# The small products of the last 64 rows for keys and queries, laid side by side on the array's row halves

## The chip, the cores and the metric

The kernel runs on one core of a Trainium2 chip. The metric is the time of one execution on the device in microseconds (us): before the change, the median of three runs is 894.02 us.

## The reference, cut to what matters

Two layers of the same pair of blocks work on x, a 2048 x 448 fp32 matrix:

```python
def _A_ref(x, wqkv, wo):                 # x has been through _layernorm
    q, k, v = (x @ wqkv) ...             # three 448 x 448 projections, 16 heads of 28
    phi = lambda t: where(t > 0, t + 1, exp(t)) + 1e-6
    kv  = einsum("bhsd,bhse->bhde", phi(k), v)
    z   = einsum("bhsd->bhd", phi(k))
    num = einsum("bhqd,bhde->bhqe", phi(q), kv)
    den = einsum("bhqd,bhd->bhq", phi(q), z) + 1e-6
    return (num / den) @ wo
def _B_ref(x, w1, b1, w2, b2):
    return gelu(x @ w1 + b1) @ w2 + b2   # 448 -> 1792 -> 448
x = x + _A_ref(_layernorm(x), ...);  x = x + _B_ref(_layernorm(x), ...)   # twice
```

The change touches only how phi(k) and phi(q) get their projections, x @ wqkv for keys and queries.

## The kernel before, in words

**Numbers in two pieces.** Every fp32 operand of a product is split into a high piece `hi` (a rounding copy to fp32r) and a low piece `lo` (what the rounding left), and a product is taken as hi·hi + hi·lo + lo·hi. The 2048 rows of x are cut into 16 tiles of 128 rows, numbered t. The 448 columns of x, which are the contraction of the projections, are cut into three chunks of 128 and a tail of 64.

**The tail.** Its 64 rows are stored twice in the transposed x, in rows 0-63 and again in rows 64-127, in the high piece as well as in the low piece. The weight of the tail, `cross` (tile `wk6` or `wq6`), holds the high piece in rows 0-63 and the low piece in rows 64-127 (`split_tail`, L97 to L100). So one matmul over 128 rows with the high piece of x gives hi·hi + hi·lo (L282), and one with the low piece gives lo·hi, together with lo·lo (L283). With three matmuls for each of three chunks (L279, L280, L281), a projection of one tile is 11 matmuls of 448 columns (`proj`).

**First half of a layer (`phase1`, L471).** For each tile t the order of the instructions is written out by hand as a string of tokens, `STEP` (L455), `STEP_0` (L456) for t = 0:

```python
STEP   = "a qp K T X s n G kp tu kh bg Q sp"
STEP_0 = "K T X kp a s kh n tu G Q bg sp"
```

On TensorE this makes, per step t: K(t), the key projection (11 matmuls, `stage_k`); T(t+1), the transposes of the next tile into a PSUM bank `tp` (four transposes, L228, only in layer 0 and only up to tile 5: `TURNED = (6, 0)`, later tiles are transposed on VectorE and through DRAM); G(t-1), 11 matmuls that add phi(k)ᵀx (L435 to L439); Q(t), the query projection (11 matmuls, `stage_q`), for t below `DEFER` = 10 only; the last six query projections stand between the two halves of a layer. The other engines follow each bank: `qp` is phi of the query of the step before, two ScalarE activations (L289, L290) and one VectorE instruction that I call eq(t-1) (L292, tile `eq`), which is the last to read the query's bank; `X` splits the transposed tile, ScalarE for the high piece XH (L234) and then VectorE for the low piece XL (L235), which K(t+1) reads; `a` and `n` are layer norm of tiles further on (L177 to L183, L356); `kp`, `kh` are phi of the key and its split.

**PSUM banks.** A pool tag has a fixed number of bank buffers. Tag "h" has two and is used by the query projection `psq` (L274) and by the transposes `tp` of layer 0; tag "m" has two and holds the key projection; tag "acc" has four and holds G. A new tile of a tag takes the buffer that came free first, and its first writer waits for the last reader of the buffer's old contents. Before the change, `psq` of step t takes the bank of `psq` of step t-1, and waits for eq(t-1); `tp` of tile t+1 takes the bank of `tp` of tile t.

The second half of a layer (the combination with wo and the MLP: `hp` L699 to L703, `y` L717 to L719) holds most of the time, is on TensorE as well, and isn't touched.

Of the kernel before, what the change touches and what calls it, by code (L numbers as in the profile page):

```python
# [10 lines left out]
F32R = mybir.dt.float32r  # L11
# [11 lines left out]
def linear_attn_mlp_kernel(  # L23
# [12 lines left out]
    pe, act, dve, pool, sp = nc.tensor, nc.scalar, nc.vector, nc.gpsimd, nc.sync  # L36
    x0 = x_in[0]
    y_out = out[0]
    S, D = x0.shape
# [22 lines left out]
    def bank(tag, bufs, name):  # L62
        return psum.tile([128, 512], F32, name=name, tag=tag, bufs=bufs)
# [7 lines left out]
    def t512(tag, bufs, name, dt=F32):  # L71
        return work.tile([128, 512], dt, name=name, tag=tag, bufs=bufs)

    def f(ap):
        return ap.bitcast(F32)
# [10 lines left out]
    wkq = {}  # L86
# [7 lines left out]
            eng.dma_start(s[64:128], src[TL:D, :])  # L94
        return s

    def split_tail(s, cross, tmp):  # L97
        act.copy(tmp, s)
        dve.tensor_copy(cross[0:64], s[0:64])
        dve.tensor_sub(cross[64:128], s[64:128], f(tmp[64:128]))  # L100

    def load_kq(name, col):
        src = wqkv[:, col:col + D]
# [18 lines left out]
    def piece(name, i):  # L122
        return t448(f"{'W' if name == 'k' else 'V'}{i}", 1, f"w{name}{i}", F32R)

    def split_kq(name, st):
        for c in range(3):
            hi = piece(name, c)
            lo = piece(name, 3 + c)
            act.copy(hi, st[c])
            if c == (0 if name == "k" else 1):  # L130
                dve.tensor_sub(lo, st[c], f(hi))
            else:
                pool.tensor_tensor(lo, st[c], f(hi), op=OP.subtract)
            wkq[name, c] = (hi, lo)
        cr = piece(name, 6)
        split_tail(st[3], cr, t512("e", 3, "sx", F32R)[:, :D])
        wkq[name, 3] = cr

    st_k = load_kq("k", D)
# [75 lines left out]
    blocks = {}  # L215
# [54 lines left out]
        dve.tensor_sub(lo.rearrange("p (c i n) -> p c i n", c=4, n=32), x, f(h))  # L270


    def proj(name, key, j):
        ps = bank("m" if name == "k" else "h", 2, "ps" + name)  # L274
        o = ps[:, :D]
        b = blocks[key]
        for c in range(3):
            hi, lo = wkq[name, c]
            pe.matmul(o, b.still(b.hi, j, c), hi, start=(c == 0), stop=False)  # L279
            pe.matmul(o, b.still(b.hi, j, c), lo, start=False, stop=False)  # L280
            pe.matmul(o, b.still(b.lo, j, c), hi, start=False, stop=False)  # L281
        pe.matmul(o, b.still(b.hi, j, 3), wkq[name, 3], start=False, stop=False)  # L282
        pe.matmul(o, b.still(b.lo, j, 3), wkq[name, 3], start=False, stop=True)  # L283
        return o

    def phi(o, name, into=None):

        e = t512("e", 3, name)[:, :D]
        act.activation(e, o, AF.Relu, scale=-1.0)  # L289
        act.activation(e, e, AF.Exp, scale=-1.0)  # L290
        into = e if into is None else into
        dve.scalar_tensor_tensor(into, o, 0.0, e, op0=OP.max, op1=OP.add)  # L292
        return into
# [99 lines left out]
    ko = {}  # L393

    def stage_k(l, t):
        ko[l, t] = proj("k", ("a", l, t // 4), t % 4)

    def stage_kphi(l, t):
        o = ko.pop((l, t))
# [13 lines left out]
            dve.tensor_tensor(za, e, za, op=OP.add)  # L413
        ks[l, t] = (kh, kl)

    qo = []

    def stage_q(l, t):
        if t is None:
            return  # L420
        qo.append((l, t, proj("q", ("a", l, t // 4), t % 4)))

    def stage_qphi():
        while qo:
# [28 lines left out]
    DEFER = NT - ORDER.split().count("Q")  # L453
# [17 lines left out]
    def phase1(l, tr):  # L471
        za = consts.tile([128, D], F32, name="za", tag="za")
        acc = [bank("acc", 4, f"G{c}")[:, :D] for c in range(4)]
        for t in range(NT):
# [3 lines left out]
            for tok in (STEP if t else STEP_0).split():  # L478
# [4 lines left out]
                elif tok == "a":  # L483
                    for u in norm:
                        stage_a(l, u)
                elif tok == "n":
                    for u in norm:
                        stage_n(l, u)
                elif tok == "tu":
                    for u in norm:  # L490
                        stage_t(l, u)
                elif tok == "T" and t + 1 < NT:
                    stage_b(l, t + 1)
                elif tok == "X" and t + 1 < NT and (l == 0 or t + 1 >= 4):
                    stage_x(l, t + 1)
                elif tok == "K":
                    stage_k(l, t)
                elif tok == "qp":
                    stage_qphi()
                elif tok == "kp":  # L500
                    stage_kphi(l, t)
                elif tok == "kh":
                    stage_kh(l, t, za)
                elif tok == "s":
                    stage_s(l, t)
                elif tok == "G" and t >= 1:
                    stage_g(l, t - 1, acc)
                elif tok == "bg" and l == 0:
                    background(BG[t])
                elif tok == "Q" and t < DEFER:  # L510
                    stage_q(l, t)
# [297 lines left out]
    stage_a(0, 0)  # L809
    stage_n(0, 0)  # L810
    split_kq("k", st_k)
    stage_b(0, 0)
    stage_x(0, 0)
    stage_a(0, 1)
    stage_n(0, 1)
    split_kq("q", st_q)
    sp.dma_start(b1s, b1.rearrange("(c p) -> p c", p=128))
    sp.dma_start(b2b, b2[None, :].to_broadcast([128, D]))

    for l in range(LAYERS):  # L820
# [6 lines left out]
        def pre(j):  # L827
# [3 lines left out]

        tok_ = SimpleNamespace(
            Q=lambda j: stage_q(l, fill.pop(0)), Qp=lambda j: stage_qphi(), G=lambda j: stage_g(l, NT - 1, acc),
            ld=lambda j: (load_pq(l, 0, j), load_x(l, j)), z=lambda j: trans_z(tr, za), gt=lambda j: trans_gt(tr, acc),
            kv=lambda j: trans_kv(tr), mask=lambda j: trans_mask(tr), m=lambda j: trans_m(tr, j),
# [4 lines left out]
        for tok in ORDER.split():  # L840
            name, j = tok.rstrip("0123456789"), int("0" + tok.lstrip("abcdefghijklmnopqrstuvwxyzQTG"))
# [5 lines left out]
        for b in range(NB):  # L847
# [6 lines left out]
            for i in range(NF):  # L854
                if i + 1 < NF:
                    mlp1(l, b, i + 1)
                elif nxt:
                    mlp1(l, b + 1, 0)
                if l == 0 and b == 0:
                    background(1)  # L860
                if nxt:
                    behind(l, b, i, tr)
                elif l + 1 < LAYERS:
                    if i == 2:
                        split_kq("k", st_k)
                    if i == 5:
                        split_kq("q", st_q)
                    if i in (3, 4, 6, 7, 8):
                        t = (3, 4, 6, 7, 8).index(i)
                        stage_a(l + 1, t)  # L870
                        stage_n(l + 1, t)
                        stage_t(l + 1, t)
                        if t % 2:
                            stage_sp(l + 1, t)
                    if 9 <= i < 13:
                        stage_x(l + 1, i - 9)
                mlp2(l, b, i, acc)
# [28 lines left out]
```

## Time and profile before

| | |
|---|---|
| median of three runs | 894.02 us (894.0 to 894.94) |
| the profiled execution's own time | 896.46 us |
| its span, first to last instruction | 894.7 us |
| mean granted TensorE clock in it | 0.996 |
| busy: TensorE, VectorE, ScalarE, GpSimd | 98%, 56%, 38%, 23% of the span |
| first half of layer 0, steps 1 to 5 | 17.57 to 54.99 us of the span |
| first half of layer 1, steps 1 to 9 | from 457.99 us of the span |

All terms of the prediction come from the profiled execution, which is 2.4 us longer than the median. In the rows of a timeline the columns are start, duration, engine, line, operation, output <- inputs, shapes, count; a bracket at the end of a row is the idle time of that engine just before the row and what ended it. PE is TensorE's matmul, PEld its weight load, DVE is VectorE, ACT ScalarE, POOL GpSimd. A matmul's recorded duration is longer than the step from one matmul to the next, because they are pipelined; the pace is read from the starts.

### The profile page before, as it was taken

The numbers are of one execution on the slowest core, as the hardware profiler recorded it, in microseconds if no ns is written. First come the engines' busy times: TensorE is split into PE (matmuls) and PEld (weight loads), VectorE is DVE, ScalarE is ACT, GpSimd is POOL, SyncE is SP. The second block draws the span as 40 slices with busy tenths as digits, with TensorE's granted clock in tenths as the row PEclk, the third lists the DMA queues.
The fourth block names the chain that finished last, engine by engine and source line by source line (L and its number), as shares of the span: only waits on it lengthen the run. The fifth ranks groups of instructions, "written<-read, shape, count | busy, mean of one in ns | idle before, by whom it ended". The sixth has DMA issues, their size and how long they took to land.

```text
span 894.7 us, 11665 instructions
## 1 busy us (share of the span) xinstructions
PE 878.8 (98%) x4184; PEld 772.8 (86%) x4184; DVE 502.3 (56%) x970; ACT 339.5 (38%) x586; POOL 209.1 (23%) x243
## 2 busy tenths in 40 slices
PE   7999999999999999999999999999999999999998
PEld 6898988888788888888889998888878888888887
DVE  6897686655754544226469866864565473532112
ACT  4677744333222322333345564343132233223221
POOL 4576723322112012002023333320310210210000
PEclk8999999999999999999999999999999999999999
DMA  6386622623513412051135542053233223010001
GB/s 175 121 244 220 194 82 92 208 76 102 170 52 92 143 33 80 16 175 48 47 127 196 173 123 82 32 178 112 65 106 132 91 92 130 34 62 20 22 1 42
DMA packets 62762, 93.71 MB, mean 105 GB/s; under 512 B 8816, under 2 KB 57968, under 8 KB 62704
## 3 DMA queue, kind: packets, MB, share of 16 engines
q1 hardware_dynamic: 62704, 92.97, 32.9%
q8 instruction: 33, 0.54, 0.3%
q14 instruction: 25, 0.20, 0.1%
HBM read 55.65 MB, written 34.08 MB: 100 GB/s over the span
## 4 chain that ended last, share of the span: by engine, by line
PE 84%; DVE 7%; issue 2%; DMA 2%; ACT 2%; POOL 2%; SPq 1%; POOLq 0%; DVEq 0%; ACTq 0%
PE y L719 10%; PE y L717 10%; PE y L718 10%; PE hp L701 8%; PE hp L700 8%; PE hp L699 8%; PE hp L703 3%; PE hp L702 3%; PE G L436 2%; PE G L437 2%; PE G L435 2%; PE op L652 2%; PE op L651 2%; PE op L653 2%; PE psk L281 2%
## 5 line engine op out<-in xcount | busy, mean ns | idle before, releaser
L709 DVE TENSOR_TENSOR gl<-g,gh 128x512 fp32r<-128x512 f32 x112 | 78.5, 701 | 303.6 <-ACT gh L708 303.5
L705 ACT ACTIVATE g<-hp,b1s 128x512 f32<-128x512 f32 x112 | 77.1, 688 | 400.7 <-PE hp L703 400.6
L717 PE MATMUL y<-w2h,gh 128*128 128x448 f32 x448 | 163.8, 366 | 1.7 <-ACT g L705 1.7
L719 PE MATMUL y<-w2h,gl 128*128 128x448 f32 x448 | 163.8, 366 | 0.5 <-DVE gl L709 0.5
L718 PE MATMUL y<-w2l,gh 128*128 128x448 f32 x448 | 163.6, 365 | 0.0
L701 PE MATMUL hp<-XL,w1h 128*128 128x512 f32 x336 | 131.3, 391 | 0.3 <-DVE XL L270 0.3
L699 PE MATMUL hp<-XH,w1h 128*128 128x512 f32 x336 | 131.5, 391 | 0.1
L700 PE MATMUL hp<-XH,w1l 128*128 128x512 f32 x336 | 131.6, 392 | 0.0
L183 POOL TENSOR_TENSOR brs<-bve,mhalf 128x1 f32<-128x1 f32 x64 | 39.8, 622 | 320.4 <-DVE bve L181 318.3
L717 PEld LDWEIGHTS y<-w2h,gh 128*128 128x128 f32 x448 | 84.1, 188 | 11.4 <-ACT g L705 2.5
L718 PEld LDWEIGHTS y<-w2l,gh 128*128 128x128 f32 x448 | 84.1, 188 | 8.3
L719 PEld LDWEIGHTS y<-w2h,gl 128*128 128x128 f32 x448 | 84.2, 188 | 7.5 <-DVE gl L709 0.9
L701 PEld LDWEIGHTS hp<-XL,w1h 128*128 128x128 f32 x336 | 63.1, 188 | 14.8 <-DVE XL L270 1.2
L699 PEld LDWEIGHTS hp<-XH,w1h 128*128 128x128 f32 x336 | 63.1, 188 | 11.8 <-ACT XH L269 0.8
L700 PEld LDWEIGHTS hp<-XH,w1l 128*128 128x128 f32 x336 | 63.1, 188 | 11.2
L708 ACT CAST gh<-g 128x512 fp32r<-128x512 f32 x112 | 69.7, 622 | 3.6
L602 POOL TENSOR_TENSOR pz<-pq,zb 128x448 f32<-128x448 f32 x32 | 37.1, 1162 | 105.2 <-DVE dn L608 74.0
L666 POOL TENSOR_TENSOR x<-x,b2b 128x448 f32<-128x448 f32 x32 | 36.9, 1152 | 31.5 <-DVE xm L190 23.3
L702 PE MATMUL hp<-XH,w1x 128*128 128x512 f32 x112 | 43.6, 389 | 0.0
L703 PE MATMUL hp<-XL,w1x 128*128 128x512 f32 x112 | 43.6, 389 | 0.0
L177 DVE BATCH_NORM_STATS2 bst<-x 128x6 f32<-128x448 f32 x64 | 39.8, 622 | 6.3 <-DMA x<-in_A_x_dram 5.2
L389 POOL TENSOR_TENSOR xnl<-x,xnh 128x384 fp32r<-128x384 f32 x32 | 35.4, 1107 | 29.6 <-ACT xnh L388 23.0
(144 smaller groups left out, 1581.1 us busy)
## 6 DMA issues: line engine op xcount, KB each, us to landing
x<-in_A_x_dram SPq DMA_DIRECT2D x32, 224.0 KB, 4.0
pq_d<-eq SPq DMA_DIRECT2D x32, 224.0 KB, 2.2
pq<-pq_d SPq DMA_DIRECT2D x32, 224.0 KB, 3.2
x<-x_d SPq DMA_DIRECT2D x32, 224.0 KB, 3.3
sq_a<-sq SPq DMA_DIRECT2D x13, 512.0 KB, 2.6
sp<-sq_a SPq DMA_DIRECT2D x52, 128.0 KB, 3.0
sq_q<-sq SPq DMA_DIRECT2D x12, 512.0 KB, 2.6
sp<-sq_q SPq DMA_DIRECT2D x48, 128.0 KB, 3.0
```

The costliest lines, as they stand in the source:

```text
L177: dve.bn_stats(st, xs)
L699: pe.matmul(o, w1h[:, c, s], x.moving(x.hi, c), start=(c == 0), stop=False)
L700: pe.matmul(o, w1l[:, c, s], x.moving(x.hi, c), start=False, stop=False)
L701: pe.matmul(o, w1h[:, c, s], x.moving(x.lo, c), start=False, stop=False)
L702: pe.matmul(o, w1x[:, s], x.moving(x.hi, 3), start=False, stop=False)
L703: pe.matmul(o, w1x[:, s], x.moving(x.lo, 3), start=False, stop=True)
L705: act.activation(g, hp, AF.Gelu_apprx_tanh, bias=b1s[:, i:i + 1])
L708: act.copy(gh, g)
L709: dve.tensor_sub(gl, g, f(gh))
L717: pe.matmul(acc[j], gh[:, s], w2h[:, i], start=first, stop=False)
L718: pe.matmul(acc[j], gh[:, s], w2l[:, i], start=False, stop=False)
L719: pe.matmul(acc[j], gl[:, s], w2h[:, i], start=False, stop=last)
```

## The change

In steps 1 to 9 of each layer, the low-times-high product of the tail, which was one 128-row matmul for the key and one for the query, becomes a 64-row matmul for each: the key's in rows 0-63, the query's in rows 64-127, one right behind the other at the end of K(t). For that, `cross` of the queries holds its high piece in rows 64-127 (the keys' stays in rows 0-63), and lo·lo, which the 128-row form added, is no longer computed in these steps. The query's bank is therefore opened (`proj_open`, first matmul with start=True) at the end of K(t) instead of at the start of Q(t). Step 0 and the six late query projections keep the old form. The number of matmuls, and of instructions on every other engine, doesn't change.

```diff
-    def split_tail(s, cross, tmp):
+    def split_tail(s, cross, tmp, hi):
+        hi, lo = (slice(0, 64), slice(64, 128)) if hi == 0 else (slice(64, 128), slice(0, 64))
         act.copy(tmp, s)
-        dve.tensor_copy(cross[0:64], s[0:64])
-        dve.tensor_sub(cross[64:128], s[64:128], f(tmp[64:128]))
+        dve.tensor_copy(cross[hi], s[hi])
+        dve.tensor_sub(cross[lo], s[lo], f(tmp[lo]))
...
-    def proj(name, key, j):
-        ps = bank("m" if name == "k" else "h", 2, "ps" + name)
-        o = ps[:, :D]
+    def proj_open(name):
+        return bank("m" if name == "k" else "h", 2, "ps" + name)[:, :D]
+
+    def proj(name, key, j, o, lo_tail=None):
...
-        pe.matmul(o, b.still(b.hi, j, 3), wkq[name, 3], start=False, stop=False)
-        pe.matmul(o, b.still(b.lo, j, 3), wkq[name, 3], start=False, stop=True)
+        pe.matmul(o, b.still(b.hi, j, 3), wkq[name, 3], start=False, stop=lo_tail == "first")
+        if lo_tail is None:
+            pe.matmul(o, b.still(b.lo, j, 3), wkq[name, 3], start=False, stop=True)
         return o
 
+    def proj_pair(key, j, k, q):
+        b = blocks[key]
+        lo = b.still(b.lo, j, 3)
+        pe.matmul(k, lo[0:64], wkq["k", 3][0:64], start=False, stop=True)
+        pe.matmul(q, lo[64:128], wkq["q", 3][64:128], start=True, stop=False)
...
     def stage_k(l, t):
-        ko[l, t] = proj("k", ("a", l, t // 4), t % 4)
+        key, j = ("a", l, t // 4), t % 4
+        pair = 1 <= t < DEFER
+        ko[l, t] = proj("k", key, j, proj_open("k"), "last" if pair else None)
+        if pair:
+            q_open[l, t] = proj_open("q")
+            proj_pair(key, j, ko[l, t], q_open[l, t])
...
     def stage_q(l, t):
...
-        qo.append((l, t, proj("q", ("a", l, t // 4), t % 4)))
+        pair = (l, t) in q_open
+        o = q_open.pop((l, t)) if pair else proj_open("q")
+        qo.append((l, t, proj("q", ("a", l, t // 4), t % 4, o, "first" if pair else None)))
```

More of the change, by code (lines that the diff above doesn't have):

```diff
@@ L135, in split_kq @@
         cr = piece(name, 6)
-        split_tail(st[3], cr, t512("e", 3, "sx", F32R)[:, :D])
+        split_tail(st[3], cr, t512("e", 3, "sx", F32R)[:, :D], 0 if name == "k" else 1)
         wkq[name, 3] = cr
@@ L278, in proj @@
             hi, lo = wkq[name, c]
-            pe.matmul(o, b.still(b.hi, j, c), hi, start=(c == 0), stop=False)
+            pe.matmul(o, b.still(b.hi, j, c), hi, start=(c == 0 and lo_tail != "first"), stop=False)
             pe.matmul(o, b.still(b.hi, j, c), lo, start=False, stop=False)
             pe.matmul(o, b.still(b.lo, j, c), hi, start=False, stop=False)
-        pe.matmul(o, b.still(b.hi, j, 3), wkq[name, 3], start=False, stop=False)
-        pe.matmul(o, b.still(b.lo, j, 3), wkq[name, 3], start=False, stop=True)
-        return o
+        pe.matmul(o, b.still(b.hi, j, 3), wkq[name, 3], start=False, stop=lo_tail == "first")
+        if lo_tail is None:
+            pe.matmul(o, b.still(b.lo, j, 3), wkq[name, 3], start=False, stop=True)
+        return o
+    def proj_pair(key, j, k, q):
[3 more added lines that the diff above has]
+        pe.matmul(q, lo[64:128], wkq["q", 3][64:128], start=True, stop=False)
     def phi(o, name, into=None):
@@ L414, in stage_kh @@
         ks[l, t] = (kh, kl)
-    qo = []
+    qo, q_open = [], {}
     def stage_q(l, t):
```

## The prediction

> **What bounds the kernel now.** I read the page first, for the busy shares and the chain that ended last, then TensorE's timeline of the first half of layer 0, then VectorE's and ScalarE's beside it.
>
> ```profile
> span 894.7 us, 11665 instructions
> PE 878.8 (98%) x4184; PEld 772.8 (86%) x4184; DVE 502.3 (56%) x970; ACT 339.5 (38%) x586; POOL 209.1 (23%) x243
> PE 84%; DVE 7%; issue 2%; DMA 2%; ACT 2%; POOL 2%; SPq 1%; POOLq 0%; DVEq 0%; ACTq 0%
> ```
>
> TensorE is the bound: 84% of the chain. So a matmul slot taken out is worth its length, and a wait put in front of TensorE is worth its length as well, unless a later wait shrinks for it. Step 2 of layer 0 in TensorE's timeline, with the starts of the next steps:
>
> ```profile
> 28.00 0.36 PE L282 MATMUL psk<-wk,XH 128*128 128x448 f32 x1
> 28.20 0.36 PE L283 MATMUL psk<-wk,XL 128*128 128x448 f32 x1
> 28.41 0.49 PE L228 MATMUL tp<-ident,x 128*128 128x128 f32 x3
> 28.76 0.45 PE L435 MATMUL G<-kh,xnh 128*128 128x448 f32 x1
> 31.72 0.47 PE L279 MATMUL psq<-wq,XH 128*128 128x448 f32 x1 [0.47 <-DVE eq L292]
> 34.05 0.36 PE L279 MATMUL psk<-wk,XH 128*128 128x448 f32 x1
> 48.30 0.36 PE L279 MATMUL psk<-wk,XH 128*128 128x448 f32 x1
> 50.53 0.36 PE L435 MATMUL G<-kh,xnh 128*128 128x448 f32 x1
> ```
>
> The pace is 0.203 us a matmul (K(5): 11 from 48.30 to 50.53). The transposes T take 0.35 us (28.41 to 28.76). The one bracket is what matters here: Q(2) waited 0.47 us for eq(1), the last reader of the query's bank. That reader is already late by a little in layer 0.
>
> **What the change takes out.** In each of 18 steps (1 to 9, two layers) two slots, 0.406 us, become one pair. What a pair costs, the trace of before can't show: no stationary or moving tile in it has 64 rows. The weight loads bound it:
>
> ```profile
> 31.71 0.19 PEld L279 LDWEIGHTS psq<-wq,XH 128*128 128x128 f32 x1 [0.85 <-DVE eq L292]
> 31.82 0.19 PEld L280 LDWEIGHTS psq<-wq,XH 128*128 128x128 f32 x1
> 28.01 0.19 PEld L283 LDWEIGHTS psk<-wk,XL 128*128 128x128 f32 x1
> ```
>
> From below: the two run in one slot with both loads hidden, 0.203. From above: each runs quite alone, load 0.19 and record 0.36, 1.10 for the two. In between: a load starts when the matmul ahead of it starts (28.01 beside 28.00), and it holds the loader for 0.11 (31.71 to 31.82). If the query's load may start only with the key's matmul, the query's matmul starts 0.11 behind it, and the pair costs 0.11 + 0.203 = 0.31. I take 0.31, the end that these rows are nearest to: a gain of 0.095 a pair (bounds: gain 0.20, loss 0.69).
>
> Two rules of the Trainium skill pull apart here. "TensorE: Matmul & The Clock Gate", in "Part 3: Packing small matmuls — row/col tiling", has matmuls on different row groups start about 4 ns apart; by that figure a pair would cost an estimated 0.207 and the sum below would be 1.4 us less. "TensorEngine Tiling (Array Packing)", in "Key Properties", says that a change of the tiling mode drains TensorE; that speaks against this change, which goes from whole rows to half rows and back in each step, and it is the third rival. No run here shows either yet.
>
> **What it moves.** Two edits are free: `split_tail` issues the same ScalarE copy and the same two 64-row VectorE instructions with the row halves exchanged, and every engine but TensorE keeps its order and its count. The costly one is the bank. In the built program of the changed kernel, the pair of step t opens the query's bank in the buffer that T(t)'s transposes left, and so T(t+1) gets the buffer of the query before, and its first transpose waits for eq(t-1), in steps 1 to 4 of layer 0. Before, Q(t) had that wait, later by T and G: 0.35 + 11 × 0.203 = 2.6 us. Behind the waiting transpose stand G(t-1), Q(t) and K(t+1) on TensorE, and on the others the split of the tile, XH and XL, and all that VectorE and ScalarE have behind it, eq(t) among it. So the wait feeds itself: T(t+1), then XL(t+1), then eq(t), then T(t+2). I follow that loop with its own lengths:
>
> ```profile
> 21.25 0.52 PE L228 MATMUL tp<-ident,x 128*128 128x128 f32 x3 [1.24 <-DVE x L356]
> 22.90 0.61 DVE L292 SCALAR_TENSOR_TENSOR eq<-psq,eq 128x448 f32<-128x448 f32 x1
> 23.43 0.68 DVE L235 TENSOR_TENSOR XL<-tp,XH 128x512 fp32r<-128x512 f32 x1
> 31.05 0.62 DVE L292 SCALAR_TENSOR_TENSOR eq<-psq,eq 128x448 f32<-128x448 f32 x1
> 31.58 0.68 DVE L235 TENSOR_TENSOR XL<-tp,XH 128x512 fp32r<-128x512 f32 x1
> 37.83 0.61 DVE L292 SCALAR_TENSOR_TENSOR eq<-psq,eq 128x448 f32<-128x448 f32 x1
> 38.36 0.68 DVE L235 TENSOR_TENSOR XL<-tp,XH 128x512 fp32r<-128x512 f32 x1
> 44.05 0.62 DVE L292 SCALAR_TENSOR_TENSOR eq<-psq,eq 128x448 f32<-128x448 f32 x1 [0.38 <-ACT eq L290]
> 29.05 0.59 ACT L234 CAST XH<-tp 128x512 fp32r<-128x512 f32 x1
> 51.15 0.62 ACT L269 CAST XH<-sp 128x512 fp32r<-128x512 f32 x1 [1.18 <-DMA sp<-sq_a]
> 51.80 0.69 DVE L270 TENSOR_TENSOR XL<-sp,XH 128x512 fp32r<-128x512 f32 x1 [1.17 <-ACT XH L269]
> ```
>
> From T to XL: XH starts 0.64 after T (28.41 to 29.05) and XL 0.65 after XH where it waits for nothing else (51.15 to 51.80), 1.29 together. From the start of XL(t+1) to the end of eq(t), by VectorE's fixed order: 23.43 to 31.67 is 8.24; 31.58 to 38.44 is 6.86; 38.36 to 44.67 is 6.31. From the end of eq to T I allow 0.05 (31.67 to the load's start 31.71). Then, with the changed kernel on the clock of the old:
>
> - T(2) waits for eq(0), which ends at 23.51: 23.56 in place of 21.25.
> - XL(2) 24.85, eq(1) ends 33.09, T(3) 33.14 in place of 28.41.
> - XL(3) 34.43, eq(2) ends 41.29, T(4) 41.34.
> - XL(4) 42.63, eq(3) ends 48.94, T(5) 48.99.
>
> T(6) doesn't exist, so the loop ends there. Behind T(5) come T 0.35, G 11 × 0.203 = 2.23 and Q(4) with one matmul less, 2.03: K(5) starts at 53.60 in place of 48.30, **5.3 us late**. In that figure the gain of steps 1 to 4 is already spent: TensorE stands idle ahead of each of the four transposes, about 3.6, 2.6, 1.2 and 0.7 us (Q(1), say, would end at 23.56 + 4.61 = 28.17 and K(2) at 28.17 + 2.34 = 30.51, 2.6 ahead of T(3)), so what a pair costs there is hidden too.
>
> **What is left of the gain.** Steps 5 to 9 of layer 0 and 1 to 9 of layer 1 have no transposes; there `psq` takes the bank of the query two steps before, whose eq is done a step earlier, and no wait is added. 14 pairs × 0.095 = 1.3 us. The rest of the first half moves as a block, VectorE with it, except one wait that TensorE's delay should swallow:
>
> ```profile
> 78.07 0.47 PE L436 MATMUL G<-kl,xnh 128*128 128x448 f32 x1 [0.42 <-DVE kl L409]
> ```
>
> VectorE comes out of the loop less late than TensorE (XL(6) at 51.80 had itself 1.17 us of room), so I count 0.4 back. The sum: 5.3 - 1.3 - 0.4 = **+3.6 us**. On the profiled execution's own 896.46 that is 900.1; carried over to the median of 894.02 it is **897.6 us**.
>
> One more term I set at nothing, with a bound. The clock was granted late once after an idle stretch:
>
> ```profile
> 9.33 0.74 PE L279 MATMUL psk<-wk,XH 128*128 128x448 f32 x1 [3.06 <-ACT XH L234]
> 11.06 0.57 PE L279 MATMUL psk<-wk,XH 128*128 128x448 f32 x1
> 13.68 0.57 PE L283 MATMUL psk<-wk,XL 128*128 128x448 f32 x1
> ```
>
> After 3.06 us of idle time, matmuls ran at (13.68 - 11.06) / 7 = 0.374, not 0.203. The idle time ahead of T(2) would be longer than that. Slow matmuls behind T(2) are covered by the 2.6 us ahead of T(3); only if the idle time ahead of T(3) slows the clock again is there something to pay: 11 × 0.17 = 1.9 us in G(1) less the 1.2 ahead of T(4), some 0.7 us.
>
> **The rivals.**
>
> - *No overlap: the change doesn't do what it says.* The pair costs two slots, 0.406: 5.3 - 0.4 = +4.9, 898.9 us. For it: each instruction of the stream has had its own slot in every row so far. Against: the two write different banks and use different rows.
> - *Not slower: the delay is paid back.* The largest waits that TensorE has behind 55 us (waited for, us in total, times, longest) are these.
>
> ```profile
> PE y L717 <- ACT g L705: 1.7, 2, 0.9
> PE tq L620 <- DVE kvm L555: 1.1, 2, 0.5
> PE G L437 <- POOL xnl L389: 0.7, 1, 0.7
> ```
>
> If these ended by the clock, by loads from DRAM for instance, a late TensorE would meet them done. All three gone besides what I count: 3.6 - 3.5 = +0.1, 894.1 us; with both loads hidden as well (0.203 a pair, 1.5 more) 892.6. It decides from 1.8 us paid back. Against it: xnl, kvm and g are made from what TensorE made just before, so they move with it.
> - *The pair drains the array twice.* A matmul's record lasts 0.36 with a pace of 0.203, 0.16 of it beyond its slot. Waiting that out on the way into the pair and out of it costs 0.32 on top of 0.203 to 0.406, so 0.52 to 0.73 a pair: 14 × 0.12 to 0.32 is a loss of 1.6 to 4.5, in all +6.5 to +9.4, 900.5 to 903.4 us. For it: the loads of a pair and of the matmul behind it can't all be done ahead in one slot. Against it: in this stream a load always ran beside the matmul ahead.
>
> **How the numbers follow.** The forecast, pair 0.2 to 0.36 and the loop as worked out (896 to 898.5): 55%. No overlap, 898.9: 15%. Drained: 18%. Paid back, 892 to 895.8: 12%. The range takes in the pair at one slot with a loop half a microsecond shorter (5.3 - 2.8 - 0.4 - 0.5 = +1.6, 895.6), some of the paid-back case below that, and at the other end the drained pair at its dearest with the clock's 0.7 (904.1): 895.0 to 904.5. A run of this kernel can tell about 0.2%, 1.8 us, from no change, so the same is 892.2 to 895.8: 12%; faster 3%; slower 85%.
>
> **What the profile of the changed kernel would show.** Layer 1's K(2) and K(3) start here before:
>
> ```profile
> 465.95 0.37 PE L279 MATMUL psk<-wk,XH 128*128 128x448 f32 x1
> 472.77 0.37 PE L279 MATMUL psk<-wk,XH 128*128 128x448 f32 x1
> ```
>
> Right: idle time of TensorE ahead of the transposes, released by eq, in steps 1 to 4 of layer 0, with T(3) near 33 and K(5) near 53.6 us; none of that in layer 1, where the step, 6.82 us before, is about 0.1 shorter; starts of the pair's two matmuls about 0.11 apart, the next matmul 0.2 behind the second. Wrong: transposes that don't wait, by which the loop falls and the kernel would be no slower; layer 1's steps longer than before, by which the pair costs more than two slots; or a gap to the old kernel that shrinks between 55 us and the end by more than the pairs give.

## The result, and the profile after

The changed kernel has a median of 903.04 us (902.11 to 904.02, four runs), the kernel before 894.01 us (893.9 to 894.94, four runs) beside it. The ratio is 1.0099 with an interval of 1.0087 to 1.0112: **9.0 us slower** (7.8 to 10.0). The forecast was +3.6, and the range ended at 904.5.

The profiled execution of the changed kernel took 902.11 us, 5.65 more than that of before (896.46). That is 3.4 less than the medians differ by: before's profiled execution lies 2.4 above its median, which the last experiment explains, and that of the changed kernel 0.9 below its own. Its page has the same shape as before, 5.7 us longer, with TensorE still the bound:

```profile
span 900.4 us, 11663 instructions
PE 881.5 (98%) x4184; PEld 769.4 (85%) x4184; DVE 502.5 (56%) x970; ACT 340.5 (38%) x586; POOL 209.5 (23%) x243
...
PE 87%; DVE 7%; ACT 2%; issue 2%; POOL 1%; DMA 1%; SPq 0%; DVEq 0%; POOLq 0%
```

Busy shares tell little here: 2.7 us more for PE, in records whose ends are modelled. The list of TensorE's waits (in total, times, longest) tells more. A new line stands on top, transposes that wait for `eq`. The waits for `g` and `kvm` that the prediction showed are what they were (1.7, and 1.0 beside 1.1); that for `xnl` has shrunk from 0.66 to 0.53, which the last experiment comes back to.

```profile
PE tp L230 <- DVE eq L304: 5.4, 3, 3.3
...
PE y L736 <- ACT g L724: 1.7, 2, 0.9
```

TensorE's timeline has both costs in it. First come the transposes T(2) to T(5) (L230) of layer 0 and starts of K (L283), then the end of K(5) with its pair (L295, L296), the second matmul of the G behind it, and K(6). The last four rows are from step 3 of layer 1: the first and the last whole-row matmul of K(3) ahead of its pair, the second matmul of G behind it, and K(4).

```profile
23.54 0.55 PE L230 MATMUL tp<-ident,x 128*128 128x128 f32 x3 [3.29 <-DVE eq L304]
...
25.00 0.57 PE L454 MATMUL G<-kh,xnh 128*128 128x448 f32 x1
...
26.12 0.57 PE L454 MATMUL G<-kh,xnh 128*128 128x448 f32 x1
...
29.86 0.37 PE L283 MATMUL psk<-wk,XH 128*128 128x448 f32 x1
...
33.43 0.55 PE L230 MATMUL tp<-ident,x 128*128 128x128 f32 x3 [0.98 <-DVE eq L304]
...
41.95 0.55 PE L230 MATMUL tp<-ident,x 128*128 128x128 f32 x3 [1.19 <-DVE eq L304]
...
49.40 0.55 PE L230 MATMUL tp<-ident,x 128*128 128x128 f32 x3
...
54.16 0.36 PE L283 MATMUL psk<-wk,XH 128*128 128x448 f32 x1
...
55.98 0.37 PE L286 MATMUL psk<-wk,XH 128*128 128x448 f32 x1
56.28 0.46 PE L295 MATMUL psk<-wk,XL 64*128 64x448 f32 x1
56.28 0.47 PE L296 MATMUL psq<-wq,XL 64*128 64x448 f32 x1
...
56.99 0.36 PE L455 MATMUL G<-kl,xnh 128*128 128x448 f32 x1
...
61.05 0.36 PE L283 MATMUL psk<-wk,XH 128*128 128x448 f32 x1
...
478.42 0.37 PE L283 MATMUL psk<-wk,XH 128*128 128x448 f32 x1
...
480.28 0.37 PE L286 MATMUL psk<-wk,XH 128*128 128x448 f32 x1
...
481.29 0.36 PE L455 MATMUL G<-kl,xnh 128*128 128x448 f32 x1
...
485.34 0.36 PE L283 MATMUL psk<-wk,XH 128*128 128x448 f32 x1
```

**The loop** is there, with T(2) at 23.54 and K(5) at 54.16 in place of 48.30: 5.86 late. On VectorE the rows of its first turn follow one another as forecast, from eq(0) to XL(2) to eq(1), whose end at 33.37 releases T(3):

```profile
22.87 0.61 DVE L304 SCALAR_TENSOR_TENSOR eq<-psq,eq 128x448 f32<-128x448 f32 x1
...
24.86 0.69 DVE L237 TENSOR_TENSOR XL<-tp,XH 128x512 fp32r<-128x512 f32 x1 [1.37 <-ACT XH L236]
...
32.76 0.61 DVE L304 SCALAR_TENSOR_TENSOR eq<-psq,eq 128x448 f32<-128x448 f32 x1
```

T(5)'s row at 49.40 has no bracket, but its weight load waited for `eq` as well. Of the 0.39 us, 0.2 is the gap that follows every pair (below), so about 0.2 is left as the wait:

```profile
49.40 0.31 PEld L230 LDWEIGHTS tp<-ident,x 128*128 128x128 f32 x3 [0.39 <-DVE eq L304]
```

**The pair** goes the other way. From the last whole-row matmul ahead of it (55.98) to the second one behind it (56.99) is 1.01 us. Two whole slots in that stretch are 0.406, so the pair takes **0.60 us**, where two whole matmuls took 0.406. The weight loads show how it comes about:

```profile
55.78 0.19 PEld L286 LDWEIGHTS psk<-wk,XH 128*128 128x128 f32 x1
...
56.27 0.18 PEld L295 LDWEIGHTS psk<-wk,XL 64*128 64x128 f32 x1 [0.31 <-issue]
56.28 0.18 PEld L296 LDWEIGHTS psq<-wq,XL 64*128 64x128 f32 x1
56.68 0.19 PEld L454 LDWEIGHTS G<-kh,xnh 128*128 128x128 f32 x1 [0.22 <-ACT xnh L400]
56.79 0.19 PEld L455 LDWEIGHTS G<-kl,xnh 128*128 128x128 f32 x1
```

The whole-row load of L286 starts at 55.78, a slot before its matmul and so beside the matmul ahead. The two half-row loads do not. L286 starts at 55.98 and its slot ends at 56.18; they start at 56.27 and 56.28, together, 0.09 behind the slot's end. Their matmuls start together too, 0.00 apart, and share one slot. Then G's whole-row load does not start beside them either: it starts 0.40 behind the pair's, which is a load of 0.11 (56.68 to 56.79), a slot of 0.20 and 0.09 again. So each change between whole rows and half rows costs about 0.09 + 0.11 = 0.20 us, and the pair costs 0.20 + 2 × 0.20 = 0.60. Overlap inside the pair is better than I took it; what I took to be hidden, the loads on either side, is not. (The bracket names a copy, xnh, as what ended this last gap of 0.22. All 14 whole-row loads behind pairs of steps without transposes have this gap, 0.21 to 0.22, with xnh, eq or "issue" (nothing that the profile shows) named as the releaser, so it isn't that copy.)

The Trainium skill's page "TensorEngine Tiling (Array Packing)", "Key Properties", says that a change of the tiling mode drains TensorE. The trace agrees in so far as each change costs 0.20 us, in which no load is done ahead; whether the array is empty then, it doesn't show. The Trainium skill's page "TensorE: Matmul & The Clock Gate", "Part 3: Packing small matmuls — row/col tiling", gives starts about 4 ns apart on different row groups; 0.00 to 0.01 here agrees with it, inside the pair.

Rows of before for the same places: K(5) at 48.30 and K(3) of layer 1 (472.77) stand in the prediction, these are their neighbours.

```profile
54.99 0.36 PE L279 MATMUL psk<-wk,XH 128*128 128x448 f32 x1
...
75.05 0.37 PE L279 MATMUL psk<-wk,XH 128*128 128x448 f32 x1
...
82.43 0.36 PE L279 MATMUL psk<-wk,XH 128*128 128x448 f32 x1
...
479.59 0.37 PE L279 MATMUL psk<-wk,XH 128*128 128x448 f32 x1
```

Step 5 of layer 0 went from 6.69 us (48.30 to 54.99) to 6.89 (54.16 to 61.05): 0.20 longer, both at the same pace. Step 3 of layer 1 went from 6.82 (472.77 to 479.59) to 6.92. That step had no wait in either kernel, and 6.82 / 33 is 0.2067 a matmul where step 5 has 6.69 / 33 = 0.2027. Before's profiled execution ran at the slower pace through the first half of layer 1, and that hid half of the pair's price. In the changed kernel the pace changes at the pair: ahead of it 0.2067 us ((480.28 - 478.42) / 9), behind it 0.2025 ((485.34 - 481.29) / 20). The last experiment counts how often.

### The profile page after: what moved, and what is told of

It is laid out like the page before. It is cut to its first block, busy times and chain, and to the rows that moved or that the text cites. A ratio compares the mean times of both kernels' runs of the same rounds, so it can differ in the third digit from the quotient of the medians.

```text
span 900.4 us, 11663 instructions
## 1 busy us (share of the span) xinstructions
PE 881.5 (98%) x4184; PEld 769.4 (85%) x4184; DVE 502.5 (56%) x970; ACT 340.5 (38%) x586; POOL 209.5 (23%) x243
## 4 chain that ended last, share of the span: by engine, by line
PE 87%; DVE 7%; ACT 2%; issue 2%; POOL 1%; DMA 1%; SPq 0%; DVEq 0%; POOLq 0%
PE y L738 10%; PE y L736 10%; PE y L737 10%; PE hp L720 8%; PE hp L719 8%; PE hp L718 8%; PE hp L722 3%; PE hp L721 3%; PE G L454 2%; PE G L456 2%; PE G L455 2%; PE psk L285 2%; PE psk L284 2%; PE psk L283 2%; PE op L671 2%
```

## The experiments

**Theory.** The loss is the sum of two costs: the loop of the early bank, some 5.3 to 5.9 us, and a pair that costs 0.20 more than two whole slots because TensorE changes twice between whole rows and half rows, 14 × 0.20 = 2.8. **Rivals:** it is the early opening as such that costs, also where no transposes wait; or each half-row matmul is slow by itself, so that its number counts and not the changes; or the halved clock behind T(2) is the cause of the later K(5) (after the 3.29 us of idle time ahead of T(2) the granted clock is 0.50 from 25 to 27 us). The first four kernels were run beside the kernel before at 895.2 us (14 runs), the last four beside it at 894.54 us (21 runs). Differences are against those.

### The pairs without the loop

```diff
-        pair = 1 <= t < DEFER
+        pair = 1 <= t < DEFER and t >= TURNED[l] - 1
```

Pairs only from step 5 of layer 0 on and in layer 1, 14 in all.

> The pairs stay only in the 14 steps in which TensorE transposes nothing (steps 5 to 9 of layer 0, 1 to 9 of layer 1), so no transpose waits for eq. Theory: each change between whole rows and half rows costs about 0.2 us, so a pair takes 0.61 in place of 0.406 and the kernel is 14 x 0.2 = 2.8 us over the one before, about 896.8, and no transpose in steps 1 to 4 waits for eq. Rival 1, the pair gains 0.1 as forecast and all of the loss is the banks': 892.7. Rival 2, pairs and whole matmuls cost alike: 894.0.

897.16 us (896.41 to 897.98, nine runs), ratio 1.0025 (1.0015 to 1.0034): +2.0. The waits for `eq` ahead of transposes are gone. The pairs alone make the kernel slower, where the forecast had them as a gain of 1.3.

### The loop without the pairs

The changed kernel with both tail products on 128 rows, each in its own slot; the order and the early bank stay.

```diff
-        pe.matmul(k, lo[0:64], wkq["k", 3][0:64], start=False, stop=True)
-        pe.matmul(q, lo[64:128], wkq["q", 3][64:128], start=True, stop=False)
+        pe.matmul(k, lo, wkq["k", 3], start=False, stop=True)
+        pe.matmul(q, lo, wkq["q", 3], start=True, stop=False)
```

(The query's `cross` has its pieces exchanged between the row halves, as in the changed kernel; over 128 rows the sum is the same.)

> The query's bank is opened at the end of K(t) as in the changed kernel, but both products are whole 128-row matmuls again, so nothing changes between whole and half rows. Theory: the loop of transposes, XL and eq is alone in it, K(5) of layer 0 about 6 us late, 0.5 of it paid back, about 899.5. Rival, the banks cost little by themselves and the pairs' price is nearly all: 895 or less.

899.83 us (899.29 to 901.4, five runs), ratio 1.0052 (1.0039 to 1.0066): +4.6. Its timeline has the loop with no half-row matmul in it:

```profile
23.60 0.90 PE L230 MATMUL tp<-ident,x 128*128 128x128 f32 x3 [3.03 <-DVE eq L304]
...
33.94 0.55 PE L230 MATMUL tp<-ident,x 128*128 128x128 f32 x3 [1.49 <-DVE eq L304]
...
54.74 0.37 PE L283 MATMUL psk<-wk,XH 128*128 128x448 f32 x1
```

K(5) is 6.4 us late in this execution, the slowest of the five (901.4). The bank causes the loop, and half rows have no part in it.

### Half rows that aren't paired

The kernel before, with the last matmul of K on rows 0-63 and that of Q on rows 64-127 in steps 1 to 9, each at its old place. lo·lo is left out there, as in the changed kernel; the query's `cross` is exchanged as in the change. 36 half-row matmuls, each alone between whole rows, and nothing else is moved.

```diff
...
-        pe.matmul(o, b.still(b.lo, j, 3), wkq[name, 3], start=False, stop=True)
+        rows = slice(0, 128) if not half_rows else slice(0, 64) if name == "k" else slice(64, 128)
+        pe.matmul(o, b.still(b.lo, j, 3)[rows], wkq[name, 3][rows], start=False, stop=True)
...
```

> The banks are as before the change; the key's 64-row matmul stands alone at the end of K(t), the query's alone at the end of Q(t), in the 18 steps. Theory: it is the change between whole and half rows that costs, 0.2 us each time, so each of 36 lone matmuls costs 0.6 in place of 0.203: 14.4 us more, about 908. Rival, a 64-row matmul costs a slot like any other and only two at once cost more: 894.

907.72 us (907.03 to 908.13, four runs), ratio 1.0139 (1.0125 to 1.0152): +12.5. A matmul with half the rows, in the old place, makes the kernel slower:

```profile
64.53 0.37 PE L283 MATMUL psq<-wq,XH 128*128 128x448 f32 x1
64.83 0.46 PE L285 MATMUL psq<-wq,XL 64*128 64x448 f32 x1
...
65.53 0.37 PE L281 MATMUL psk<-wk,XH 128*128 128x448 f32 x1
```

From the whole matmul ahead to the second one behind is 1.00 us (64.53 to 65.53), the same as with a pair. One half-row matmul costs 0.60, and so do two side by side. The price is that of going there and back; the second matmul rides along. That the whole is 12.5 and not 36 × 0.40 = 14.4 lies mostly in the steps with waits: K(1) to K(5) of layer 0 took 32.29 us (17.93 to 50.22) in place of 30.73, 1.6 more, where four steps at 0.8 would be 3.2.

### The pair twice

The kernel of the first experiment, with each pair issued two times in a row, so that its low-times-high product is counted twice. If half-row matmuls are slow in themselves, it costs 0.40 to 0.60 more a step; if the changes are, one slot of 0.20 more.

```diff
-        pe.matmul(k, lo[0:64], wkq["k", 3][0:64], start=False, stop=True)
-        pe.matmul(q, lo[64:128], wkq["q", 3][64:128], start=True, stop=False)
+        for i in range(2):
+            pe.matmul(k, lo[0:64], wkq["k", 3][0:64], start=False, stop=i == 1)
+            pe.matmul(q, lo[64:128], wkq["q", 3][64:128], start=i == 0, stop=False)
...
```

> As the run with 14 pairs without transposes, but each pair is issued twice in a row (the low-times-high product of the tail is added twice, so the sums differ from the reference's). Theory: the second pair changes nothing between whole and half rows and costs one slot, 0.203 to 0.22: about 3 us over that run, 899.8. Rival, every pair costs its 0.6: 8.5 us over that run, 905.

898.43 us (897.91 to 900.05, five runs), ratio 1.0038 (1.0025 to 1.005): +3.2, 1.3 more than with single pairs.

```profile
57.11 0.37 PE L286 MATMUL psk<-wk,XH 128*128 128x448 f32 x1
57.40 0.47 PE L296 MATMUL psk<-wk,XL 64*128 64x448 f32 x1
...
57.71 0.35 PE L296 MATMUL psk<-wk,XL 64*128 64x448 f32 x1
...
58.32 0.36 PE L456 MATMUL G<-kl,xnh 128*128 128x448 f32 x1
```

```profile
58.01 0.19 PEld L455 LDWEIGHTS G<-kh,xnh 128*128 128x128 f32 x1 [0.31 <-ACT XH L271]
```

The stretch is 1.21 us (57.11 to 58.32) in place of 1.01: the second pair adds one slot, 0.20. The whole-row load behind it comes 0.30 after the second pair's matmuls start (57.71 to 58.01), a slot and 0.09 as before; the bracket now names XH and no longer xnh. The median rose by 1.3 where 14 × 0.20 gives 2.8, a miss in size. The rows of the step decide between changes and matmuls. In the profiled executions of the two kernels the steps with pairs (K(5) to K(10) of layer 0, K(1) to K(10) of layer 1) together took 99.91 us here and 97.80 with single pairs, 2.1 more: single pairs also switch the pace, as the last experiment tells, and doubled ones seldom do. Where the rest went was not settled.

### The changed kernel again

> The changed kernel itself, on the chip of the runs beside it. Theory of two causes that add up: the loop of the early bank (4.6 us in the run with whole rows) and 14 changes to half rows and back (2.0 us in the run with 14 pairs) give 6 to 8 us over the kernel before. If it is 9 again, something of 1 to 2 us is in it that neither run has.

902.77 us (902.59 to 903.94, four runs), ratio 1.0098 (1.0084 to 1.0111): +8.2, a little above what was expected. The parts, +2.0 and +4.6, make 6.6 together, 1.6 less. The three intervals leave about a microsecond either way each, so that they can hold the difference; what it is was not settled.

### The idle time of step 1 filled

The changed kernel with the query's half-row product issued 14 more times in step 1 of layer 0, each as a start of its own that overwrites the one before; TensorE is then busy where it waited 3.29 us for eq(0).

```diff
-        pe.matmul(q, lo[64:128], wkq["q", 3][64:128], start=True, stop=False)
+        for n in range(1 + fill):
+            pe.matmul(q, lo[64:128], wkq["q", 3][64:128], start=True, stop=n < fill)
...
```

> The changed kernel, with the query's 64-row product in step 1 of layer 0 issued 14 times more into the same bank (each starts the bank anew, so the result is the same): some 2.8 us of work in the 3.3 us that TensorE waits for eq(0). Theory: the clock then isn't halved in the matmuls behind the first late transpose, G(0) goes back from 3.9 to 2.2 us, and the loop, which runs over VectorE and ScalarE, gets at most 0.3 to 0.5 us shorter: K(5) of layer 0 at about 53.7 in place of 54.16, the kernel 0 to 0.6 us faster than the changed one. Rival, the halved clock is a main part of the loss: K(5) 1.7 us or more earlier.

902.88 us (902.5 to 902.97, four runs), ratio 1.0095 (1.0082 to 1.0109): as without the filling.

```profile
28.23 0.36 PE L283 MATMUL psk<-wk,XH 128*128 128x448 f32 x1
...
33.38 0.55 PE L230 MATMUL tp<-ident,x 128*128 128x128 f32 x3 [2.55 <-DVE eq L305]
...
54.10 0.36 PE L283 MATMUL psk<-wk,XH 128*128 128x448 f32 x1
```

In the changed kernel the idle time ahead of T(2) was followed by matmuls at (26.12 - 25.00) / 3 = 0.373 us, at a granted clock of 0.50 (25 to 27 us), and K(2) came at 29.86. Filled, the granted clock is 1.00 there, K(2) comes at 28.23, 1.6 us earlier; and T(3) then waits 2.55 for eq(1) where it waited 0.98. K(5) stands at 54.10 beside 54.16, where 53.7 was expected. The slowed clock costs nothing, because the loop's wait lies behind it.

### 96 rows in place of 64

The kernel before, with the last matmul of K and of Q on rows 0-95 in steps 1 to 9; half of lo·lo is left out.

```diff
...
-        pe.matmul(o, b.still(b.lo, j, 3), wkq[name, 3], start=False, stop=True)
+        n = 96 if part_rows else 128
+        pe.matmul(o, b.still(b.lo, j, 3)[0:n], wkq[name, 3][0:n], start=False, stop=True)
...
```

> As the kernel before, but in the 18 steps the last matmul of key and query takes rows 0 to 95 only (low times high and a third... half of low times low, which is below the rounding). The array isn't divided for it: its tile is still 128 by 128. Theory: it is the division into half-row tiles that costs, not rows that stay empty: 895, as before, and no gap around these matmuls. Rival, any matmul with fewer rows than the one before it costs 0.4 more: about 908.

895.83 us (895.41 to 896.58, ten runs), ratio 1.002 (1.0011 to 1.0029): +1.3, against +12.5 for 64 rows.

```profile
48.55 0.37 PE L279 MATMUL psk<-wk,XH 128*128 128x448 f32 x1
...
55.05 0.36 PE L284 MATMUL psq<-wq,XL 96*128 96x448 f32 x1
55.25 0.37 PE L279 MATMUL psk<-wk,XH 128*128 128x448 f32 x1
```

The recorded tile is 96*128, and not 128 by 128 as expected. The matmul behind it starts one slot later, 0.20, and the step is 6.70 us (before 6.69). At the matmul itself fewer rows cost nothing in these rows; 64 rows do. Why the median is 1.3 us higher they don't show; the profiled execution had the most of the slower pace that the last section tells of, 2.3 us.

### Opening early without transposes and without half rows

The kernel of the first experiment, with both tail products on 128 rows as in the second.

> The query's bank opened early in the 14 steps without transposes alone, with whole 128-row products: neither half rows nor a transpose that waits. Theory: opening early is free there, 0 to 0.5 us from the kernel before. Rival, the early bank costs in these steps too: 1 us or more over it, and the price of the 14 pairs would be that much smaller.

893.9 us (893.09 to 896.99, eleven runs), ratio 0.9998 (0.9987 to 1.0009): no difference. Opening the query's bank early costs nothing that these runs can tell (about a microsecond either way) where no transposes wait. The first experiment is 2.6 us above this one when each is taken against the kernel before that ran beside it (3.3 in bare medians, from two groups of runs); 14 pairs with two changes each would cost 14 × 0.20 = 2.8.

The traces give the price by steps. From K(5) to K(10) of layer 0 the changed kernel took 34.64 us and this one 33.44, from K(2) to K(10) of layer 1 55.52 and 53.50: 3.2 us for 13 pairs, 0.25 each. The pair in step 1 of layer 1 cost nothing: the step took 7.70 us beside 7.68, because G waits in it for `xnl`, and that wait shrank. The first row is this kernel's, the second the changed kernel's:

```profile
461.03 0.47 PE L456 MATMUL G<-kh,xnl 128*128 128x448 f32 x1 [0.66 <-POOL xnl L401]
...
467.49 0.48 PE L456 MATMUL G<-kh,xnl 128*128 128x448 f32 x1 [0.53 <-POOL xnl L401]
```

What a pair costs above 0.20 is the pace behind it. In the four profiled executions with single pairs (the changed kernel twice, filled, and without the loop), 44 of these 13 × 4 pairs have the whole-row matmuls at about 0.203 us on one side and at about 0.2066 on the other, so that nearly every other step runs at the slower pace; of the 13 doubled pairs, 2 do. Why a single pair switches the pace stays open.

This run is also the better base for an account of the trace, since its profiled execution lies at its median (893.87), while before's lay 2.4 above its own. One part of what was special in that one is the slower pace in layer 1 (6.82 a step beside 6.69 here), the other is seen in step 9. TensorE in this kernel, and VectorE in this kernel:

```profile
75.05 0.37 PE L283 MATMUL psk<-wk,XH 128*128 128x448 f32 x1
...
81.74 0.36 PE L283 MATMUL psk<-wk,XH 128*128 128x448 f32 x1
```

```profile
71.32 0.63 DVE L179 BATCH_NORM_STATS2 bst<-x 128x6 f32<-128x448 f32 x1 [2.28 <-DMA x<-in_A_x_dram]
...
76.83 0.58 DVE L426 SCALAR_TENSOR_TENSOR kl<-psk,kh 128x448 fp32r<-128x448 f32 x1
```

And VectorE in the kernel before:

```profile
71.93 0.63 DVE L177 BATCH_NORM_STATS2 bst<-x 128x6 f32<-128x448 f32 x1 [1.81 <-DMA x<-in_A_x_dram]
...
77.44 0.58 DVE L409 SCALAR_TENSOR_TENSOR kl<-psk,kh 128x448 fp32r<-128x448 f32 x1
```

K(9) stands at 75.05 in both. But kl came at 77.44 in before's profiled execution and comes at 76.83 here, and the step takes 6.69 in place of 7.38. VectorE waits for a load of x in both, and goes on at 71.93 there and at 71.32 here, 0.61 earlier; in the 96-row kernel, which has the order of the kernel before, it is 71.32 as well. So the wait of 0.42 for kl, on which I built a term, belonged to one execution in which a load came late, and not to the kernel.

No version that beats the kernel before came out of this. By these prices, pairs that follow one another in one go cost 0.40 for the two changes and 0.20 each, against 0.406 each for whole slots: even at two pairs, and by this estimate a gain from three on. Three would need three open query banks beside three of the key, and tags "h" and "m" have two each; that wasn't tried.

## Why the prediction was wrong

The sign was right, and it came from the loop, as forecast. The size was not: +9.0 in place of +3.6. That the range held the time is owed to its upper end, which was set by a rival that the forecast didn't follow, and no merit of the sum.

- **The step that failed is the price of a pair**, the term "14 pairs × 0.095 = 1.3" of gain. A pair took 0.60 and not 0.31, so that by the rows of the pair the term is a loss of 14 × 0.20 = 2.8. By the steps of the trace, with the pace in them and one pair hidden in a wait, it is a loss of 3.2: 4.5 us of the miss of 5.4. I bounded the pair by two rows of loads in a stream of equal shapes, where a load always runs beside the matmul ahead, and carried that over to a change of shape. The loads between shapes run beside nothing. My third rival, "the pair drains the array twice", is what comes nearest, at the middle of its price (0.52 to 0.73), and it stood at 18%. It put the cost at each change, where it is, but took it for 0.16 from the end of a matmul's record; measured are 0.09 and a load of 0.11. Its "for" was right word for word: the loads of the pair and of the matmul behind it can't be done ahead. Its "against" was a statement on a stream in which the case doesn't occur. The sign that I had given for it, layer 1's steps longer than before, is there, 6.92 beside 6.82. The prediction also held two paces without using it: 0.203 us a matmul in K(5), and 6.82 / 33 = 0.2067 in layer 1.
- **The loop of the early bank** was right in cause and course, as the whole-row version and the version without transposes show. T(2) to T(5) came at 23.54, 33.43, 41.95 and 49.40, forecast at 23.56, 33.14, 41.34 and 48.99; K(5) came 5.86 late and not 5.3. Two stretches of VectorE from XL to the end of eq were 0.27 and 0.29 longer than before (24.86 to 33.37 is 8.51, not 8.24), which the filled version shows not to be the clock; the third was 0.24 shorter. From T(5) to K(5) were 4.76 us, not 4.61. Idle time of 3.29, 0.98 and 1.19 us ahead of T(2) to T(4) hid what the pairs cost there, as forecast; ahead of T(5), where I had 0.7, about 0.2 was left.
- **The 0.4 paid back** rested on a wait of one execution. Against a base without it, nothing of that came back. Behind the pairs of layer 0 some 0.6 us seems to come back: the changed kernel's K(10) starts 7.06 behind that of the last experiment (88.80 and 81.74), its K(0) of layer 1 6.45 behind (459.30 and 452.85). But in the second profiled execution of the changed kernel these are 7.34 and 7.23, and the stretch from the one to the other differs by up to 1.5 us between the profiled executions at hand. So it isn't shown that anything was paid back.
- **The halved clock at nothing** was right: K(5) within 0.06 us with and without it.
- Of the other rivals, "no overlap" is refuted by the pair's starts (56.28 and 56.28) and by the second pair's 0.20. "Paid back" is refuted for g and kvm, whose waits stayed, so that they moved with TensorE, as I had argued. For xnl I was wrong in part: its wait shrank and took in the pair of that step (7.70 us beside 7.68).

The account with measured terms: loop 5.9 and pairs 3.2, in all +9.1. In the trace K(10) of layer 1 starts 8.49 us behind that of the last experiment (526.98 and 518.49), and the last matmul 8.23 behind (896.42 and 888.19); the 0.9 between lies in stretches that the change doesn't touch. The median of the changed kernel, in the second group of runs, is 8.9 above that experiment's, and it is 9.0 and 8.2 above the kernel before in the two comparisons. What remains, up to 0.9 us, is of the size by which single executions vary.

## What to carry to other kernels

Packing small matmuls side by side on row halves is paid per visit and not per matmul: price the two changes of shape first (0.40 us here, two slots of 448 columns), and by these prices pack only where three or more pairs follow one another, which no run here tried. Before an accumulation is opened earlier, look at which buffer of its pool the next tile then gets: a bank handed to the transposes of the next tile turned a wait of 0.47 us into a loop of 5.9. And a wait that a term of the sum rests on should be looked for in a second execution first.

## What the runs showed that was not expected

- **One half-row matmul costs as much as a pair, 0.60 us, and a matmul on 96 rows costs one slot.** The recorded tile (64*128 beside 96*128 and 128*128) tells the two apart.
- **Two paces at a full granted clock.** In the first halves, whole-row matmuls of 448 columns run at 0.203 us for some stretches and at 0.207 for others, from one step to tens of microseconds long and in other places in each execution: 6.69 and 6.82 us for steps of 33 matmuls without a wait in one and the same execution of the kernel before, at a granted clock of 1.00 in both (37 to 44 and 472 to 479 us). Single pairs mostly switch between the two, but streams of whole rows have both as well. Added up over the steps of at most 0.215 us between such matmuls in the first halves, the excess over 0.2025 us comes to 0.3 to 2.3 us an execution in the profiles at hand. The cause stays open; it is enough to move a single profiled execution by the size of a term.
